# Attention scores of the last 64 keys as float32 64x64 products, with side work of the attention loop moved

## The chip, the cores and the metric

The kernel runs on one core of one Trainium2 chip. The metric is the device time of one execution in microseconds (us); lower is better. Three runs of the kernel before took 912.76 to 914.37 us, median 913.71 us. A profile of one further execution gives the trace that is read here.

## The reference

Attention with a sigmoid in place of the softmax, then a mixture-of-experts layer with greedy routing by capacity:

```python
B, H, S, D = 8, 12, 448, 64                       # float32 q, k, v
scores = q @ k.transpose(0, 1, 3, 2) / sqrt(D) - log(S)
attn_out = (1 / (1 + exp(-scores))) @ v           # per image and head
x = attn_out.transpose(0, 2, 1, 3).reshape(3584, 768)
logits = x @ w_gate                               # 8 experts
# (token, expert) pairs in the order of falling logits: a token goes to its
# first expert that has room; each expert takes 3584 / 8 = 448 tokens
for e in range(8):
    out[mask[e]] = relu(x[mask[e]] @ w1[e]) @ w2[e]   # 768 -> 1024 -> 768
```

## The kernel before

The program has three stages, one behind the other: attention with the gate's logits (to about 304 us of the profiled span), routing for the first expert (to about 358 us), and the experts' products, between which the routing for the later experts runs. All instructions are issued in the order of the code: each engine works through its own queue in that order and waits on semaphores. The change touches the first stage alone.

**The attention loop.** The work is cut into 48 pairs of heads (8 images of 6 pairs; "odd" and "even" below are by the pair's number in its image). Step `i` of the loop holds, in this order: `load` of the pairs `i+4` and `i+5` (even steps only), `turn` of pair `i+1`, the `scores` of pair `i`, up to two functions off the list `bg`, and `av` of pair `i-1`.

- `load(b, g)` issues the DMAs of four heads. For each of the two pairs, 4 DMAs bring k and 4 bring q into one tile `nkq` [128, 2, 448] (4 buffers), k from SP's queue and q from GpSimd's (POOL's); 6 more bring v (`nv`, `nr`; 3 buffers each). For the first two pairs q comes over ACT's queue and v over POOL's.
- `turn` is one 32x32 block transpose of k and q on DVE into `kqT` (float32; the partitions hold 2 heads of 64 channels, the two slots of the next axis are k and q). The function `split` that it returns makes the fp32r pair: `kqH` (rounded, ACT) and `kqL` (`kqT - kqH`, DVE). `split` is called behind the first scores of a step, so ACT does the first sigmoid `at`, then `kqH`, then the other sigmoids.
- `scores(c)` for 128 keys makes six fp32r products (high times high, high times low, low times high, for two heads on the two row halves of the array) into a tile `sc` of two PSUM banks (3 buffers), and ACT turns it into `at` (8 buffers) with one sigmoid of 896 columns.
- 448 keys are three and a half such groups. An odd pair makes a fourth tile, for the last 64 keys of two pairs: six products with the last 128 keys of the pair before, of which only the upper 64 rows stay, then six with the last 64 keys of its own over the lower 64 rows. So `kqH` and `kqL` of the pair before (2 buffers each) are read until the end of an odd step.
- `av` multiplies v with the sigmoids in plain float32 in the form 128x64 (`L441`), and for an odd pair the shared fourth tile with the last 64 rows of v, in the form 64x64 (`L447`), into the PSUM tiles `tp` (2 buffers). DVE copies the result to `xt` (`L449`) and for odd pairs adds the other part (`L451`).
- `bg` holds `logits` of a whole image (24 products 128x32, then an addition on DVE) and, for the first image only, 8 pieces `rows` (three transposes into `tp`, a copy on DVE, and behind every second piece a store). The rows of the other seven images come after the loop.
- `route_consts` makes the constants of the routing: 16 iotas and memsets on POOL and 25 small operations on DVE (shifts, comparisons, casts), all at the end of step 2, behind that step's `av`.

Of the kernel before, what the change touches and what calls it, by code (L numbers as in the profile page):

```python
# [47 lines left out]
def route_consts(nc, cp, K):  # L48
# [6 lines left out]
    nc.vector.tensor_scalar(t1, t1, 4, None, OP.logical_shift_right)  # L55
# [5 lines left out]
    nc.vector.tensor_scalar(K.G, t1, t10, None, OP.is_equal)
# [3 lines left out]
    nc.vector.tensor_scalar(K.TRI, ti, 128.5, None, OP.is_gt)  # L65
# [11 lines left out]
    nc.vector.tensor_copy(K.rank, t3)  # L77
# [254 lines left out]
def moe_attention(tc, q, k, v, w_gate, w1, w2, out):  # L332
# [7 lines left out]
    with contextlib.ExitStack() as ctx:  # L340
# [21 lines left out]
        def load(b, g, qq=nc.gpsimd, vq=nc.sync):  # L362


            nat["v", b, g] = ld.tile([128, G4, 3, D], F32, name="nv", bufs=3)
            nat["r", b, g] = ld.tile([128, 2, D], F32, name="nr", bufs=3)
            for i in range(2):
                t = nat["kq", b, 2 * g + i] = ld.tile([128, 2, S // 32, 32], F32, name="nkq", bufs=4)
                for n, (qn, src) in enumerate(((nc.sync, k), (qq, q))):
                    for j in range(2):  # L370
                        rws = src[b, g * G4 + 2 * i + j].rearrange("(c p) (x d) -> x p c d", p=32, x=2)
                        for x in range(2):
                            o = 64 * j + 32 * x
                            qn.dma_start(t[o:o + 32, n], rws[x])  # L374
# [11 lines left out]
        load(0, 0, nc.scalar, nc.gpsimd)  # L386
# [6 lines left out]
        KQ = {}  # L393
        def turn(b, pr):


            T = wk.tile([128, 2, S], F32, name="kqT")
            nc.vector.transpose(T.rearrange("p n t -> p (n t)"), nat["kq", b, pr].rearrange("p n c d -> p (n c d)"))  # L398
# [4 lines left out]
            def split():
                nc.scalar.activation(H, T, AF.Copy)  # L404
                nc.vector.tensor_tensor(L, T, H.bitcast(F32), OP.subtract)  # L405
            return split
# [3 lines left out]
        def products(p, b, pr, keys, m):  # L410


            KH, KL, QH, QL = KQ[b, pr]
            for i, (R, M) in enumerate(((KH, QH), (KH, QL), (KL, QH))):
                for j, half in enumerate((LO, HI)):
                    nc.tensor.matmul(p[:m, j, :S], R[half, keys], M[half], start=i == 0, stop=i == 2)  # L416

        def scores(b, pr, c):


# [7 lines left out]
            nc.scalar.activation(a, p[:, :, :S], AF.Sigmoid, bias=bias, scale=1 / math.sqrt(D))  # L428
# [376 lines left out]
```

## Time and profile before

| | before |
|---|---|
| runs, us | 912.76, 913.71, 914.37 |
| profiled execution, us | 915.77 |
| its span, first to last instruction, us | 914.0 |
| mean granted TensorE clock | 0.984 |
| busy PE / DVE / ACT / POOL | 94% / 59% / 50% / 51% |

| stretch of the span, us | PE busy | DVE busy | ACT busy | POOL busy | DMA share |
|---|---|---|---|---|---|
| 0 to 9 (first loads) | 0.18 | 1.32 | 2.33 | 8.20 | 0.96 |
| 9 to 304 (attention) | 286.07 | 151.73 | 198.22 | 117.61 | 0.56 |
| 304 to 398 (routing, first expert begins) | 72.62 | 80.25 | 46.22 | 28.71 | 0.59 |
| 398 to 914 (experts) | 501.81 | 301.83 | 210.90 | 309.14 | 0.39 |

A row of the timeline gives the start in us from the span's start, the duration, the engine, the line, the operation, the tiles (out<-in) and, in square brackets, the idle time of the engine before it and what ended that. One product in float32 is recorded as two matmuls, one in fp32r as one. Neighbours of one kind are merged into a row with a count; their durations overlap, so what a matmul costs is read from the distance between starts.

### The profile page before, as it was taken

What the parts mean: (1) busy time and instruction counts of PE and PEld (TensorE: products, weight loads), DVE (VectorE), ACT (ScalarE), POOL (GpSimd) and SP (SyncE); (2) the same over time, 40 slices, a digit from 0 to 9 for tenths busy, and PEclk for the clock granted to TensorE, in tenths of its full rate; (3) what the DMA queues carried; (4) which work ended last, traced back from release to release, by engine and by line L of the source; (5) the groups of instructions that cost most, each with busy time, mean ns of one, the idle gap of its engine ahead of it and who ended that gap; (6) DMA issues with size and microseconds to landing.
All of it is one profiled execution on the core that took longest, in us unless ns stands there. A gap on an engine that the chain in (4) does not pass through costs nothing.

```text
span 914.0 us, 16457 instructions
## 1 busy us (share of the span) xinstructions
PE 860.7 (94%) x5603; PEld 656.2 (72%) x5603; DVE 535.1 (59%) x2053; ACT 457.7 (50%) x633; POOL 463.7 (51%) x442
## 2 busy tenths in 40 slices
PE   5898999999999774998999999999999999999997
PEld 3444555555555444987998888988988888989996
DVE  3645455555554588876968969959779632330110
ACT  5565676676677472443433534534434434544441
POOL 8533444444430003573675675684784783741651
PEclk9999999999999996999899999999999999999999
DMA  9646665555550486324434343353452442632421
GB/s 176 140 97 149 126 128 117 116 125 118 116 121 1 127 277 185 108 82 149 140 114 146 122 147 124 128 151 113 154 162 96 141 154 90 213 117 82 158 76 61
DMA packets 205236, 117.59 MB, mean 129 GB/s; under 512 B 145728, under 2 KB 194880, under 8 KB 205152
## 3 DMA queue, kind: packets, MB, share of 16 engines
q1 hardware_dynamic: 190688, 83.03, 35.2%
q0 software_dynamic: 10752, 33.05, 11.4%
q10 hardware_dynamic: 3712, 0.46, 0.3%
q8 instruction: 44, 0.72, 0.3%
q14 instruction: 40, 0.33, 0.1%
HBM read 94.47 MB, written 22.02 MB: 127 GB/s over the span
## 4 chain that ended last, share of the span: by engine, by line
PE 78%; DVE 11%; issue 4%; DMA 2%; POOL 2%; ACT 2%; SPq 0%; POOLq 0%; ACTq 0%; DVEq 0%
PE sc L416 14%; PE tp L441 12%; PE sc L671 9%; PE sc L669 9%; PE sc L673 9%; PE sc L706 6%; PE sc L708 6%; PE sc L704 6%; DVE r_junk L170 3%; PE tp L447 2%; PE tp L634 2%; PE tp L621 2%; DMA xr<-xs,r_idx 1%; PE tp L462 1%; POOL wl L587 1%
## 5 line engine op out<-in xcount | busy, mean ns | idle before, releaser
L587 POOL TENSOR_TENSOR wl<-wr,wh 128x768 fp32r<-128x768 f32 (+1 forms) x96 | 205.7, 2151 | 135.5 <-ACT wh L585 124.6
L428 ACT ACTIVATE at<-sc,bias 128x896 f32<-128x896 f32 x168 | 160.6, 1003 | 63.2 <-PE sc L416 62.9
L374 POOL DMA_DIRECT2D nkq<-in_q_dram x184 | 115.5, 640 | 142.3 <-DVE kqT L398 132.9
L708 PE MATMUL sc<-hh,wl 128*128 128x448 f32 (+2 forms) x400 | 151.4, 379 | 0.0
L673 PE MATMUL sc<-xh,wl 128*128 128x448 f32 (+2 forms) x396 | 146.7, 370 | 0.0
L671 PE MATMUL sc<-xl,wh 128*128 128x448 f32 (+2 forms) x396 | 146.3, 370 | 0.0
L706 PE MATMUL sc<-hl,wh 128*128 128x448 f32 (+2 forms) x400 | 145.5, 364 | 0.2 <-POOL hl L681 0.2
L669 PE MATMUL sc<-xh,wh 128*128 128x448 f32 (+2 forms) x396 | 145.4, 367 | 0.0
L704 PE MATMUL sc<-hh,wh 128*128 128x448 f32 (+2 forms) x400 | 143.9, 360 | 0.0
L170 DVE TENSOR_SCALAR_CACHE_REDUCE r_junk<-r_KE,r_T 128x224 bf16<-128x224 f32 x315 | 123.3, 442 | 0.1
L441 PE MATMUL tp<-at,nv 128*64 128x448 f32 x576 | 118.8, 548 | 4.8 <-DVE xr L478 4.4
L585 ACT ACTIVATE wh<-wr 128x768 fp32r<-128x768 f32 (+1 forms) x112 | 102.0, 939 | 9.7 <-DMA wr<-in_moe_w_dram 9.7
L405 DVE TENSOR_TENSOR kqL<-kqT,kqH 128x896 fp32r<-128x896 f32 x48 | 52.4, 1092 | 68.5 <-ACT kqH L404 68.5
L681 POOL TENSOR_TENSOR hl<-yt,hh 128x896 fp32r<-128x896 f32 x32 | 68.2, 2132 | 46.7 <-ACT yt L680 45.1
L416 PE MATMUL sc<-kqH 64*128 64x448 f32 (+1 forms) x384 | 79.3, 410 | 11.7 <-ACT kqH L404 8.8
L677 ACT ACTIVATE hh<-sc 128x896 fp32r<-128x896 f32 x32 | 29.4, 919 | 111.5 <-PE sc L673 111.5
L441 PEld LDWEIGHTS tp<-at,nv 128*64 128x64 f32 x576 | 37.0, 136 | 63.7 <-issue 55.3
L706 PEld LDWEIGHTS sc<-hl,wh 128*128 128x128 f32 x400 | 75.2, 188 | 7.3 <-issue 1.1
L671 PEld LDWEIGHTS sc<-xl,wh 128*128 128x128 f32 x396 | 75.5, 191 | 6.5 <-issue 0.4
L669 PEld LDWEIGHTS sc<-xh,wh 128*128 128x128 f32 x396 | 75.7, 191 | 5.7
L607 POOL DMA_INDIRECT xr<-xs,r_idx x32 | 31.9, 997 | 94.0 <-ACT wh L585 83.2
L673 PEld LDWEIGHTS sc<-xh,wl 128*128 128x128 f32 x396 | 75.5, 191 | 5.0
(155 smaller groups left out, 1327.3 us busy)
## 6 DMA issues: line engine op xcount, KB each, us to landing
wr<-in_moe_w_dram SPq DMA_DIRECT2D x64, 384.0 KB, 3.0
wr<-in_moe_w_dram SPq DMA_DIRECT2D x48, 512.0 KB, 3.9
nkq<-in_k_dram SPq DMA_DIRECT2D x192, 56.0 KB, 2.5
xs<-xr SPq DMA_DIRECT2D x32, 336.0 KB, 3.3
nkq<-in_q_dram POOLq DMA_DIRECT2D x184, 56.0 KB, 2.6
nv<-in_v_dram SPq DMA_DIRECT2D x92, 96.0 KB, 2.4
nr<-in_v_dram SPq DMA_DIRECT2D x46, 32.0 KB, 2.3
xr<-xs,r_idx POOLq DMA_INDIRECT x32, 4.6
```

Of the source, the lines that this page charges most:

```text
L170: nc.vector.tensor_scalar(junk, KE, T[:, i:i + 1].bitcast(F32), None, OP.is_ge, OP.add, accum_out=cnt[:, i:i + 1])
L374: qn.dma_start(t[o:o + 32, n], rws[x])
L416: nc.tensor.matmul(p[:m, j, :S], R[half, keys], M[half], start=i == 0, stop=i == 2)
L428: nc.scalar.activation(a, p[:, :, :S], AF.Sigmoid, bias=bias, scale=1 / math.sqrt(D))
L441: nc.tensor.matmul(p[j * 64:j * 64 + 64, :S], nat["v", b, g][:, h0 + j, c, :], AT[b, pr, c][:, j, :], start=(c == 0), stop=(c == 2 and pr ...
L587: eng.tensor_tensor(lo, raw[u], hi.bitcast(F32), OP.subtract)
L669: nc.tensor.matmul(ph[:, f, lo:hi], wh[:, a, fs], xh[:, dd, lo:hi], start=st, stop=False)
L671: nc.tensor.matmul(ph[:, f, lo:hi], wh[:, a, fs], xl[:, dd, lo:hi], start=False, stop=False)
L673: nc.tensor.matmul(ph[:, f, lo:hi], wl[:, a, fs], xh[:, dd, lo:hi], start=False, stop=en)
L704: nc.tensor.matmul(py[:, d2, :w], wh[:, a, dsl], h1, start=st, stop=False)
L706: nc.tensor.matmul(py[:, d2, :w], wh[:, a, dsl], h2, start=False, stop=False)
L708: nc.tensor.matmul(py[:, d2, :w], wl[:, a, dsl], h1, start=False, stop=(j == 1 and a == 3))
```

## The change

Six things are done.

1. The fourth tile is made by a function of its own, `rest_scores`, from the float32 `kqT` of two pairs: four plain float32 products of 64 keys, one for each quarter of the array. It is called at the end of the even step before (behind that step's `av`), so its sigmoid stands on ACT between two steps. `kqT` gets 3 buffers in place of 2.
2. `bg` is worked off behind `av` (and behind `rest_scores`) in place of ahead of it, one function in each step in place of two.
3. `route_consts` is a generator: its POOL part runs in step 3, its DVE part in six pieces at the ends of steps 5 to 10.
4. The first pair's transpose, `kqH` and `kqL` are made in two halves (k, then q).
5. In the first `load`, q of the second pair comes over POOL's queue in place of ACT's, and there ahead of v.
6. With that, no step reads the `kqH` and `kqL` of the pair before any more.

```diff
@@ route_consts: all DVE operations now stand behind the POOL ones @@
+    yield
+    yield
+    nc.vector.tensor_scalar(t1, t1, 4, None, OP.logical_shift_right)
+    nc.vector.tensor_scalar(t9, t9, 4, None, OP.logical_shift_right)
+    nc.vector.tensor_copy(t10, t9)
+    yield
+    nc.vector.tensor_scalar(K.G, t1, t10, None, OP.is_equal)
+    nc.vector.tensor_scalar(K.TRI, ti, 128.5, None, OP.is_gt)
+    yield
+    nc.vector.tensor_copy(K.rank, t3)
...
+    yield
+    nc.vector.tensor_scalar(K.SEL, t6, t7, None, OP.is_equal)
     for st in range(1, 16):
...
+        if st % 5 == 0:
+            yield
@@ moe_attention @@
-        def load(b, g, qq=nc.gpsimd, vq=nc.sync):
+        def load(b, g, qq=(nc.gpsimd, nc.gpsimd), vq=nc.sync):
...
-                for n, (qn, src) in enumerate(((nc.sync, k), (qq, q))):
+                for n, (qn, src) in enumerate(((nc.sync, k), (qq[i], q))):
...
-        load(0, 0, nc.scalar, nc.gpsimd)
+        load(0, 0, (nc.scalar, nc.gpsimd), nc.gpsimd)
...
-        def turn(b, pr):
+        def turn(b, pr, cuts=((0, 2),)):
-            T = wk.tile([128, 2, S], F32, name="kqT")
-            nc.vector.transpose(T..., nat["kq", b, pr]...)
+            T = KT[b, pr] = wk.tile([128, 2, S], F32, name="kqT", bufs=3)
+            for x, y in cuts:
+                nc.vector.transpose(T[:, x:y]..., nat["kq", b, pr][:, x:y]...)
...
             def split():
-                nc.scalar.activation(H, T, AF.Copy)
-                nc.vector.tensor_tensor(L, T, H.bitcast(F32), OP.subtract)
+                for x, y in cuts:
+                    nc.scalar.activation(H[:, x:y], T[:, x:y], AF.Copy)
+                    nc.vector.tensor_tensor(L[:, x:y], T[:, x:y], H[:, x:y].bitcast(F32), OP.subtract)
...
-            if c < 3:
-                products(p, b, pr, slice(c * 128, c * 128 + 128), 128)
-            else:
-                products(p, b, pr - 1, slice(S - 128, S), 128)
-                products(p, b, pr, slice(S - 64, S), 64)
+        def rest_scores(b, pr):
+            a = AT[b, pr, 3] = wk.tile([128, 2, S], F32, name="at", bufs=AT_BUFS)
+            p = ps_s.tile([128, 2, 512], F32, name="sc")
+            for o, T in ((HI, KT[b, pr - 1]), (LO, KT[b, pr])):
+                for j, half in enumerate((LO, HI)):
+                    nc.tensor.matmul(p[o, j, :S], T[half, 0, S - 64:S], T[half, 1], start=True, stop=True)
+            sigmoid(a, p)
...
-        turn(*pairs[0])()
+        turn(*pairs[0], ((0, 1), (1, 2)))()
         bg, late = [], []
+        consts = route_consts(nc, cp, K)
...
-            for c in range(4 if cur and cur[1] % 2 else 3 if cur else 0):
+            for c in range(3 if cur else 0):
                 scores(*cur, c)
                 if c == 0 and split:
                     split()
-            for _ in range(2):
-                if bg:
-                    bg.pop(0)()
+            if bg and not cur:
+                bg.pop(0)()
             if old:
                 av(*old)
-            if i == 2:
-                route_consts(nc, cp, K)
+            if cur and cur[1] % 2 == 0:
+                rest_scores(*nxt)
+            if i > 2:
+                next(consts, None)
+            if bg and cur:
+                bg.pop(0)()
```

**Where the instructions stand, 1: TensorE (PE).** Step 7 of the kernel before (an odd pair: its first three score tiles, of which the last stands in the first three rows, then the fourth tile with `kqH_541` of the pair before and `kqH_623` of its own; the logits of image 0 and a piece of its rows; then `av`):

```order
L416 MATMUL sc_693<-kqH_623 128x448 x2
L416 MATMUL sc_693<-kqL_624,kqH_623 128x448 x2
L416 MATMUL sc_693<-kqH_623,kqL_624 128x448 x2
L416 MATMUL sc_702<-kqH_541 128x448 x2
L416 MATMUL sc_702<-kqL_542,kqH_541 128x448 x2
L416 MATMUL sc_702<-kqH_541,kqL_542 128x448 x2
L416 MATMUL sc_702<-kqH_623 64x448 x2
L416 MATMUL sc_702<-kqL_624,kqH_623 64x448 x2
L416 MATMUL sc_702<-kqH_623,kqL_624 64x448 x2
L462 MATMUL tp_716<-xt_265,wgz_84 32x112 x24
L473 MATMUL tp_743<-ident_81,xt_265 112x128 x3
L441 MATMUL tp_749<-at_625,nv_274 64x448 x2
```

The end of step 8 of the kernel after (an even pair: the last score tile's last rows would stand ahead; here the last of `av`, its 64x64 part, the new fourth tile of step 9, a piece of rows, and the first scores of step 9):

```order
L455 MATMUL tp_765<-at_657,nv_269 64x448 x2
L461 MATMUL tp_772<-at_624,nr_270 64x448
L461 MATMUL tp_765<-at_624,nr_270 64x448
L461 MATMUL tp_772<-at_624,nr_270 64x448
L461 MATMUL tp_765<-at_624,nr_270 64x448
L441 MATMUL sc_780<-kqT_633 64x448 x2
L441 MATMUL sc_780<-kqT_732 64x448 x2
L487 MATMUL tp_793<-ident_81,xt_260 112x128 x3
L431 MATMUL sc_803<-kqH_734 128x448 x2
L431 MATMUL sc_803<-kqL_735,kqH_734 128x448 x2
L431 MATMUL sc_803<-kqH_734,kqL_735 128x448 x2
```

Twelve fp32r products ahead of an odd pair's `av` are gone; four float32 products stand behind an even step's 64x64 part of `av`, and the side work stands behind them.

**2: ScalarE (ACT)** from the start of the program, before (q's DMAs for pairs 0 and 1, the table load, then `kqH` and sigmoids of the steps 0 and 1):

```order
L374 DMA nkq_94<-in_q_dram 32x14x32 x4
L374 DMA nkq_103<-in_q_dram 32x14x32 x4
L387 ACT_TABLE_LOAD
L387 ACTIVATE warm_85<-warm_85 1x1
L404 ACTIVATE kqH_154<-kqT_152 128x896
L428 ACTIVATE at_188<-sc_189,bias_82 128x896
L404 ACTIVATE kqH_186<-kqT_184 128x896
L428 ACTIVATE at_199<-sc_200,bias_82 128x896
L428 ACTIVATE at_208<-sc_209,bias_82 128x896
L428 ACTIVATE at_221<-sc_222,bias_82 128x896
L404 ACTIVATE kqH_219<-kqT_217 128x896
```

And after:

```order
L381 DMA nkq_94<-in_q_dram 32x14x32 x4
L394 ACT_TABLE_LOAD
L394 ACTIVATE warm_85<-warm_85 1x1
L414 ACTIVATE kqH_155<-kqT_152 128x448 x2
L421 ACTIVATE at_191<-sc_192,bias_82 128x896
L414 ACTIVATE kqH_189<-kqT_187 128x896
L421 ACTIVATE at_202<-sc_203,bias_82 128x896
L421 ACTIVATE at_211<-sc_212,bias_82 128x896
L421 ACTIVATE at_220<-sc_221,bias_82 128x896
L421 ACTIVATE at_231<-sc_232,bias_82 128x896
L414 ACTIVATE kqH_229<-kqT_227 128x896
```

Four DMAs are gone from ACT's queue, and `at_220`, the fourth tile's sigmoid, now stands ahead of the first sigmoid and of `kqH` of the odd step (`at_231`, `kqH_229`).

**3: VectorE (DVE)**, the end of step 2 and the start of step 3, before (the copies of `av`, then constants, the first ones and the last, and the transpose for pair 4):

```order
L449 COPY xt_265<-tp_333 128x448
L451 TENSOR_TENSOR xt_265<-tp_340,xt_265 128x448
L55 TENSOR_SCALAR c_t1_350<-c_t1_350 128x128
L59 TENSOR_SCALAR c_t9_353<-c_t9_353 128x1
L60 CAST c_t10_354<-c_t9_353 128x1
L61 TENSOR_SCALAR c_G_347<-c_t1_350,c_t10_354 128x128
L65 TENSOR_SCALAR c_TRI_361<-c_ti_348 128x128
```

After, the same place and the steps 3 to 5:

```order
L463 COPY xt_260<-tp_328 128x448
L465 TENSOR_TENSOR xt_260<-tp_335,xt_260 128x448
L406 STREAM_TRANSPOSE kqT_349<-nkq_163 128x896
L415 TENSOR_TENSOR kqL_352<-kqT_349,kqH_351 128x896
L463 COPY xt_260<-tp_382 128x448
L406 STREAM_TRANSPOSE kqT_453<-nkq_172 128x896
L415 TENSOR_TENSOR kqL_456<-kqT_453,kqH_455 128x896
L463 COPY xt_260<-tp_486 128x448
L465 TENSOR_TENSOR xt_260<-tp_493,xt_260 128x448
L406 STREAM_TRANSPOSE kqT_507<-nkq_271 128x896
L415 TENSOR_TENSOR kqL_510<-kqT_507,kqH_509 128x896
L463 COPY xt_260<-tp_540 128x448
```

No constant stands between the copies of step 2 and the next transpose any more.

More of the change, by code (lines that the diff above doesn't have):

```diff
@@ L54, in route_consts @@
     nc.gpsimd.iota(t1, [[1, 128]], base=0, channel_multiplier=0)
-    nc.vector.tensor_scalar(t1, t1, 4, None, OP.logical_shift_right)
     t9 = cp.tile([128, 1], I32, name="c_t9")
@@ L64, in route_consts @@
     K.TRI = cp.tile([128, 128], BF, name="c_TRI")
-    nc.vector.tensor_scalar(K.TRI, ti, 128.5, None, OP.is_gt)
     K.ones = cp.tile([128, 1], BF, name="c_ones")
@@ L76, in route_consts @@
     nc.gpsimd.iota(t3, [[-1, 8]], base=8, channel_multiplier=0)
-    nc.vector.tensor_copy(K.rank, t3)
     K.tok = cp.tile([112, 32], F16, name="c_tok")
@@ L90, in route_consts @@
     nc.gpsimd.iota(t5, [[0, 1]], base=0, channel_multiplier=1)
-    nc.vector.tensor_scalar(t5, t5, 31, None, OP.bitwise_and)
     nc.gpsimd.iota(t6, [[1, 2], [2, 4]], base=0, channel_multiplier=0)
-    t7 = cp.tile([128, 1], F32, name="c_t7")
-    nc.vector.tensor_copy(t7, t5)
-    nc.vector.tensor_scalar(K.SEL, t6, t7, None, OP.is_equal)
     K.kk = cp.tile([128, 16, 3], I32, name="c_kk")
@@ L99, in route_consts @@
     nc.gpsimd.iota(t8, [[1, 3]], base=1, channel_multiplier=0)
+    K.c0 = cp.tile([128, 3], I32, name="c_c0")
+    for i, u in enumerate((0xBFFFFFFF, 0x00000000, 0x40000000)):
+        nc.gpsimd.memset(K.c0[:, i:i + 1], _s32(u))
+    yield
[8 more added lines that the diff above has]
+    nc.vector.tensor_copy(K.rank, t3)
+    nc.vector.tensor_copy(K.tok, t4)
+    nc.vector.tensor_scalar(t5, t5, 31, None, OP.bitwise_and)
+    t7 = cp.tile([128, 1], F32, name="c_t7")
+    nc.vector.tensor_copy(t7, t5)
+    yield
+    nc.vector.tensor_scalar(K.SEL, t6, t7, None, OP.is_equal)
     g = 0
@@ L104, in route_consts @@
         g ^= (0x4B000000 << sh) & 0xFFFFFFFF
+        if st % 5 == 0:
+            yield
     K.gfin = _s32(g)
-    K.c0 = cp.tile([128, 3], I32, name="c_c0")
-    for i, u in enumerate((0xBFFFFFFF, 0x00000000, 0x40000000)):
-        nc.gpsimd.memset(K.c0[:, i:i + 1], _s32(u))
 class Router:
@@ L391, in moe_attention @@
             nc.sync.dma_start(wgz[:, :, s, 8 * s:8 * s + 8], w_gate.rearrange("(c p) e -> p c e", p=128))
-        KQ = {}
-        def turn(b, pr):
-            T = wk.tile([128, 2, S], F32, name="kqT")
-            nc.vector.transpose(T.rearrange("p n t -> p (n t)"), nat["kq", b, pr].rearrange("p n c d -> p (n c d)"))
+        KQ, KT = {}, {}
+        def turn(b, pr, cuts=((0, 2),)):
+            T = KT[b, pr] = wk.tile([128, 2, S], F32, name="kqT", bufs=3)
+            for x, y in cuts:
+                nc.vector.transpose(T[:, x:y].rearrange("p n t -> p (n t)"),
+                                    nat["kq", b, pr][:, x:y].rearrange("p n c d -> p (n c d)"))
             H = wk.tile([128, 2, S], F32R, name="kqH")
@@ L403, in split, with sigmoid, scores @@
             def split():
-                nc.scalar.activation(H, T, AF.Copy)
-                nc.vector.tensor_tensor(L, T, H.bitcast(F32), OP.subtract)
+                for x, y in cuts:
+                    nc.scalar.activation(H[:, x:y], T[:, x:y], AF.Copy)
+                    nc.vector.tensor_tensor(L[:, x:y], T[:, x:y], H[:, x:y].bitcast(F32), OP.subtract)
             return split
         AT = {}
-        def products(p, b, pr, keys, m):
+        def sigmoid(a, p):
+            nc.scalar.activation(a, p[:, :, :S], AF.Sigmoid, bias=bias, scale=1 / math.sqrt(D))
+        def scores(b, pr, c):
+            a = AT[b, pr, c] = wk.tile([128, 2, S], F32, name="at", bufs=AT_BUFS)
+            p = ps_s.tile([128, 2, 512], F32, name="sc")
             KH, KL, QH, QL = KQ[b, pr]
@@ L415, in products @@
                 for j, half in enumerate((LO, HI)):
-                    nc.tensor.matmul(p[:m, j, :S], R[half, keys], M[half], start=i == 0, stop=i == 2)
-        def scores(b, pr, c):
-            a = AT[b, pr, c] = wk.tile([128, 2, S], F32, name="at", bufs=AT_BUFS)
+                    nc.tensor.matmul(p[:, j, :S], R[half, c * 128:(c + 1) * 128], M[half], start=i == 0, stop=i == 2)
+            sigmoid(a, p)
+        def rest_scores(b, pr):
+            a = AT[b, pr, 3] = wk.tile([128, 2, S], F32, name="at", bufs=AT_BUFS)
             p = ps_s.tile([128, 2, 512], F32, name="sc")
-            if c < 3:
-                products(p, b, pr, slice(c * 128, c * 128 + 128), 128)
-            else:
-                products(p, b, pr - 1, slice(S - 128, S), 128)
-                products(p, b, pr, slice(S - 64, S), 64)
-            nc.scalar.activation(a, p[:, :, :S], AF.Sigmoid, bias=bias, scale=1 / math.sqrt(D))
+            for o, T in ((HI, KT[b, pr - 1]), (LO, KT[b, pr])):
+                for j, half in enumerate((LO, HI)):
+                    nc.tensor.matmul(p[o, j, :S], T[half, 0, S - 64:S], T[half, 1], start=True, stop=True)
+            sigmoid(a, p)
         XT = {}
```

4 lines of the change are left out of this document (removed).

## The prediction

> **What bounds the kernel now.** First the page: how busy TensorE is, and whose work makes the chain that ended last.
>
> ```profile
> span 914.0 us, 16457 instructions
> ...
> PE 860.7 (94%) x5603; PEld 656.2 (72%) x5603; DVE 535.1 (59%) x2053; ACT 457.7 (50%) x633; POOL 463.7 (51%) x442
> ...
> PE   5898999999999774998999999999999999999997
> ...
> PE 78%; DVE 11%; issue 4%; DMA 2%; POOL 2%; ACT 2%; SPq 0%; POOLq 0%; ACTq 0%; DVEq 0%
> ```
>
> PE carries 78% of the chain, and the slices of the attention stage (the first 13) are full of it, but for the first. So a step of the attention loop lasts as long as PE's queue for it, and I priced the change from distances between PE's starts. Next came the timeline of one odd and one even step:
>
> ```profile
> 153.91 0.47 PE L416 MATMUL sc<-kqH 64*128 64x448 f32 x2
> ...
> 155.66 0.37 PE L416 MATMUL sc<-kqH,kqL 64*128 64x448 f32 x2
> ...
> 155.95 0.47 PE L416 MATMUL sc<-kqH 64*128 64x448 f32 x2
> ...
> 157.36 2.48 PE L441 MATMUL tp<-at,nv 128*64 128x448 f32 x12
> ...
> 159.76 0.47 PE L416 MATMUL sc<-kqH 64*128 64x448 f32 x2
> ...
> 160.74 1.01 ACT L428 ACTIVATE at<-sc,bias 128x896 f32<-128x896 f32 x1 [0.18 <-PE sc L416]
> ...
> 161.49 0.36 PE L416 MATMUL sc<-kqH,kqL 64*128 64x448 f32 x2
> ...
> 161.78 2.48 PE L441 MATMUL tp<-at,nv 128*64 128x448 f32 x12
> ...
> 161.91 0.95 ACT L404 ACTIVATE kqH<-kqT 128x896 fp32r<-128x896 f32 x1 [0.16 <-ACT at L428]
> ...
> 162.89 1.09 DVE L405 TENSOR_TENSOR kqL<-kqT,kqH 128x896 fp32r<-128x896 f32 x1 [1.37 <-ACT kqH L404]
> ...
> 164.19 0.98 PE L447 MATMUL tp<-at,nr 64*64 64x448 f32 x8
> ...
> 165.10 0.47 PE L416 MATMUL sc<-kqH 64*128 64x448 f32 x2
> ```
>
> The odd step runs from 153.91 to 159.76 (5.85), the even one to 165.10 (5.34); in the odd one the fourth tile lies between 155.95 and 157.36. In the even one, three score tiles take 2.02 (to 161.78), `av` 2.41, the 64x64 part 0.91.
>
> **The fourth tile.** Without it an odd step is three score tiles and `av`: 2.02 + 2.40 (157.36 to 159.76) = 4.42, so 5.85 − 4.42 = 1.43 goes. Its replacement has no row of its own, but `L447` has its form: four float32 products 64x64, two for each row half, two for each column half, 448 columns, the row halves writing different banks. All four take 0.91 with the change of form on both sides. Their inner distance:
>
> ```profile
> 153.00 0.98 PE L447 MATMUL tp<-at,nr 64*64 64x448 f32 x8
> ...
> 153.42 0.56 PE L447 MATMUL tp<-at,nr 64*64 64x448 f32 x4
> ...
> 154.05 0.62 DVE L449 COPY xt<-tp 128x448 f32<-128x448 f32 x1 [1.53 <-PE tp L447]
> ...
> 155.12 1.10 DVE L398 STREAM_TRANSPOSE kqT<-nkq 128x896 f32<-128x896 f32 x1
> ```
>
> The second four of eight records start 0.42 after the first, and the next scores 0.49 after those. Standing right behind `L447` in the same form, the new tile needs two such distances: 2 × 0.42 = 0.84 at most, 2 × 0.375 = 0.75 if it goes on like `av`, whose six distances fill 2.25 of its 2.40. I take 0.80; the ends for the range are 0.75 and 0.91. Each of 24 double steps changes by 0.80 − 1.43 = −0.63; one of them lies in the start below, so 23 × 0.63 = **−14.5**.
>
> Does anything take PE's place? Let an odd step begin at 0. ACT now has the fourth tile's sigmoid first: it can start some 0.2 behind the last product and ends at 1.2; the first sigmoid (ready at 0.98, as 160.74 − 159.76) ends at 2.15; `kqH` (0.95) ends at 3.2 with its gap of 0.16; `kqL` (1.09) at 4.35. The transpose it needs ends at about 1.6: in the rows the copy starts 0.14 behind the 64x64 part and the transpose ends 2.17 after that, and 0.75 of this lies behind the new tile. The next step begins at 4.42, and `kqL` is wanted 0.31 later (its second kind of product): 0.4 to spare. ACT's load in a double step, seven sigmoids and two `kqH` at 0.95 to 1.01, is at most 9 of 10.56. The `sc` buffer that the third score tile wants, 1.33 into the odd step, is freed at 1.2. SP and POOL get no more DMAs in the loop; k and q come three pairs ahead. All hidden, the narrowest cover being that 0.4.
>
> **The constants.** The timeline around step 2, whose end holds them:
>
> ```profile
> 25.14 0.47 PE L416 MATMUL sc<-kqH 64*128 64x448 f32 x2
> ...
> 26.35 2.14 DVE L55 TENSOR_SCALAR c_t<-c_t 128x128 int32<-128x128 int32 x1
> ...
> 27.28 1.00 POOL L85 MEMSET c_mv<- 112x1024 f16 x1
> ...
> 28.74 0.29 DVE L61 TENSOR_SCALAR c_G<-c_t,c_t 128x128 bf16<-128x128 int32 x1
> ...
> 30.86 1.10 DVE L398 STREAM_TRANSPOSE kqT<-nkq 128x896 f32<-128x896 f32 x1
> ...
> 33.98 0.64 PE L416 MATMUL sc<-kqH 64*128 64x448 f32 x2 [2.92 <-ACT at L428]
> ...
> 37.54 2.48 PE L441 MATMUL tp<-at,nv 128*64 128x448 f32 x12
> ...
> 40.86 0.47 PE L416 MATMUL sc<-kqH 64*128 64x448 f32 x2
> ```
>
> From 26.35 to 30.86 DVE does constants, the transpose comes late, and PE stands idle for 2.92 before the scores at 33.98. That step lasts 33.98 − 25.14 = 8.84 in place of 5.85. The step behind it lasts 6.88 in place of 5.34, all of it in its scores, which need 3.56 in place of 2.02: PE is slow again after the pause. Both losses, 2.99 + 1.54, should go: **−4.5**. The new pieces hold at most three operations of 0.29 or six small ones, some 0.6 per step, behind copies where DVE has 0.5 or more before `kqH` wants the transpose; I cost them at nothing, and if that cover is short, at 0.1 to 0.3 in each of six steps.
>
> [...] The operation of 2.14 us ends just after POOL's memset (27.28 + 1.00), while one of the same size takes 0.29. [...]
>
> [...]
>
> ```profile
> L374 POOL DMA_DIRECT2D nkq<-in_q_dram x184 | 115.5, 640 | 142.3 <-DVE kqT L398 132.9
> ```
>
> **Logits and rows.** The five steps with the first image's side work:
>
> ```profile
> 52.05 0.47 PE L416 MATMUL sc<-kqH 64*128 64x448 f32 x2
> ...
> 55.50 1.36 PE L462 MATMUL tp<-xt,wgz 128*32 128x112 f32 x48
> 56.79 0.54 PE L473 MATMUL tp<-ident,xt 128*112 128x128 f32 x3
> ...
> 87.10 0.54 PE L473 MATMUL tp<-ident,xt 128*112 128x128 f32 x3
> 87.57 2.48 PE L441 MATMUL tp<-at,nv 128*64 128x448 f32 x12
> 89.98 0.48 PE L416 MATMUL sc<-kqH 64*128 64x448 f32 x2
> ```
>
> ```profile
> PE tp L441 <- DVE xr L478: 4.4, 3, 1.6
> ```
>
> They take 37.93; three plain odd and two plain even steps would take 3 × 5.85 + 2 × 5.34 = 28.23. Of the other 9.70, logits are 1.29 (55.50 to 56.79) and eight rows at 0.47 (87.10 to 87.57) are 3.76; 4.65 is waiting, and the waits table names it: `av` wants a `tp` buffer that a copy of rows still holds. Behind `av`, one piece a step, the copy has the next step's scores (2.02) to finish in. In an even step the piece itself may have to wait for the copy of the first `tp`, which ends 0.76 behind the 64x64 part, covered by the new tile's 0.80. I leave 0.05 for each of eight: **−4.2** (3.0 to 4.65). Logits of all images cost the same 1.29 behind `av` as ahead of it.
>
> **The start.**
>
> ```profile
> 6.28 1.11 DVE L398 STREAM_TRANSPOSE kqT<-nkq 128x896 f32<-128x896 f32 x1 [6.28 <-DMA nkq<-in_q_dram]
> ...
> 8.82 0.74 PE L416 MATMUL sc<-kqH 64*128 64x448 f32 x2 [8.82 <-ACT kqH L404]
> ...
> 10.32 1.11 DVE L398 STREAM_TRANSPOSE kqT<-nkq 128x896 f32<-128x896 f32 x1 [0.44 <-DMA nkq<-in_k_dram]
> ...
> 19.80 0.47 PE L416 MATMUL sc<-kqH 64*128 64x448 f32 x2
> ```
>
> The first transpose waits for q. In halves the k part runs before that, so from 6.28 there remain half a transpose (0.55) and half a `kqH` (0.47), with the hand-overs about 7.7 in place of 8.82. But pair 1's transpose at 10.32 waits for k while the DMA engines are full (share 0.96 up to 9 us), and the change issues k no earlier; it then gates `kqH`, the fourth tile and step 1. Going on by these durations (ACT: `kqH` to 12.4, three sigmoids and the fourth to 16.2, `kqH` to 17.1; PE's `av` from 15.95) I get step 2 at 18.5 in place of 19.80: **−1.3**, between −2.5 (k lands earlier, as ACT's queue is done sooner) and +1.5 (pair 2's q, now behind pair 1's 4 DMAs and v on POOL, lands late).
>
> **Sum.** 14.5 + 4.5 + 4.2 + 1.3 = 24.5, none of it in the later stages, which begin that much earlier with the same work. The profiled execution took 915.77 (1.77 outside its span of 914.0), 2.06 above the median of the runs; the span should come to 889.5, and the time, from the median of 913.71, to 889.2. I say 889.3.
>
> **The rivals.**
> - *`kqL` late in odd steps.* Speaking for it: only 0.4 to spare behind a sigmoid that was not there. If `kqH` slips by one more activation (0.95), each of 23 odd steps stalls by 0.55: +12.7, 902. Against: each duration in that sum is measured. Half of such a slip gives about 891 to 896.
> - *The four products share the array only in pairs*, like `av` (0.40 for each two records): 1.60, +0.17 per double step in place of −0.63; 23 × 0.80 = 18.4 above the forecast, 907.7. Against: `L447`.
> - *Slower than before: the four run one behind another.* Eight records at 0.40 make 3.20; the double step grows by 1.77, 24 × 1.77 = 42.5, less the 10.0 of the other parts: 946. It decides from 1.43 + 10.0 / 24 = 1.85 per tile on. For it, only that these operands, `kqT` twice, have never been read so; against, that `L447` has 0.91 in all its 24 places.
> - *The start gains nothing or loses 1.5*: 890.5 to 892.
> [...]
>
> **How the numbers follow.** Forecast 0.66, late `kqL` 0.13, pairs 0.03, one by one 0.03, start 0.09, constants 0.06. The forecast's own range is 886.5 (tile at 0.75: 15.7; rows 4.65; constants 4.5; start 2.5) to 893 (tile at 0.84, rows 3.0, start 0). Start and constants lie inside it; with the milder half of the late `kqL` and a tile at 0.91 the range becomes 886 to 896.5 and leaves out somewhat under 2 in 10. A measurement of this kernel can tell about 0.2%, 1.8 us, from no change: faster 0.95, same 0.02, slower 0.03.
>
> **What would show it.** In the profile after: even steps of about 6.1 and odd ones of 4.4, the four `kqT` products taking 0.75 to 0.85; no idle PE near 31 to 34 us and no slow scores behind it; no wait of `av` for a copy of rows; step 2's scores at 18 to 19 us; the attention's last 64x64 part near 279 us in place of 303. It is wrong if odd steps wait for `kqL`, if the `kqT` products start more than 0.45 apart, or if the routing behind gives time back.

## The result, and the profile after

Four runs of the changed kernel took 886.94 to 890.47 us, median 888.97; the kernel before took 914.04 beside them (912.76 to 914.58). The ratio is 0.9726, 95% interval 0.97 to 0.9752. The forecast was 889.3.

The profiled execution took 887.7 us. From its page: span and counts, the busy engines, PE's 40 slices, and the shares of the chain that ended last.

```profile
span 885.9 us, 16254 instructions
...
PE 843.1 (95%) x5507; PEld 638.0 (72%) x5507; DVE 534.8 (60%) x2055; ACT 457.1 (52%) x634; POOL 466.1 (53%) x446
...
PE   6999999999998739998999999999999999999996
...
PE 79%; DVE 11%; issue 5%; POOL 3%; DMA 1%; ACT 0%; SPq 0%; POOLq 0%; DVEq 0%
```

PE's work fell by 17.6 us (860.7 before), and its share of the chain stayed where it was. The dip inside the first slices is gone. The attention stage ended 26.1 us earlier: its last 64x64 part of `av` starts at 302.54 in the kernel before and at 276.42 after. The stretches behind it, cut 26.1 earlier than in the table of before (the columns are length, then busy PE, PEld, DVE, ACT and POOL, granted clock, DMA share, GB/s):

```profile
277.90:371.90 94.00, 72.76 (x472) 58.21 (x473) 80.41 (x430) 46.43 (x84) 28.87 (x19) 0.91 0.59 185
371.90:885.90 514.00, 500.15 (x2821) 442.71 (x2819) 301.59 (x1419) 210.99 (x331) 309.03 (x208) 0.99 0.40 127
```

Routing has the same busy times as before. The experts end 2.0 us earlier in this trace, but from the first expert's product to the end all the traces of this study lie between 551.3 and 555.4, with the same code there: scatter. So the rest of this text goes by where attention ends. The medians differ by 25.1.

One odd and one even step of the timeline after:

```profile
158.96 0.47 PE L431 MATMUL sc<-kqH 64*128 64x448 f32 x2
159.18 1.91 ACT L421 ACTIVATE at<-sc,bias 128x896 f32<-128x896 f32 x2 [1.75 <-PE sc L441]
...
160.24 0.19 PEld L431 LDWEIGHTS sc<-kqH 64*128 64x128 f32 x2 [0.17 <-ACT at L421]
160.28 0.42 PE L431 MATMUL sc<-kqH 64*128 64x448 f32 x2
...
160.97 0.95 ACT L414 ACTIVATE kqH<-kqT 128x896 fp32r<-128x896 f32 x1
...
161.95 1.09 DVE L415 TENSOR_TENSOR kqL<-kqT,kqH 128x896 fp32r<-128x896 f32 x1 [1.43 <-ACT kqH L414]
...
163.44 0.47 PE L431 MATMUL sc<-kqH 64*128 64x448 f32 x2
163.75 0.36 PE L431 MATMUL sc<-kqL,kqH 64*128 64x448 f32 x2
...
167.87 0.98 PE L461 MATMUL tp<-at,nr 64*64 64x448 f32 x8
168.67 0.93 PE L441 MATMUL sc<-kqT 64*64 64x448 f32 x8
169.53 0.47 PE L431 MATMUL sc<-kqH 64*128 64x448 f32 x2
```

The odd step takes 4.48, the even one 6.09, together 10.57 (10.58 as a mean; 11.19 before). The four `kqT` products start 0.80 behind the 64x64 part of `av`, and the next scores 0.86 behind them.

The constants and the rows, in the timeline:

```profile
27.50 0.47 PE L431 MATMUL sc<-kqH 64*128 64x448 f32 x2
...
33.59 0.47 PE L431 MATMUL sc<-kqH 64*128 64x448 f32 x2
...
38.73 0.22 DVE L94 TENSOR_SCALAR c_t<-c_t 128x128 int32<-128x128 int32 x1
...
49.94 0.47 PE L431 MATMUL sc<-kqH 64*128 64x448 f32 x2
...
56.10 0.54 PE L487 MATMUL tp<-ident,xt 128*112 128x128 f32 x3
56.57 0.47 PE L431 MATMUL sc<-kqH 64*128 64x448 f32 x2
```

Step 4 runs from 27.50 to 33.59, a plain even step; the constant that took 2.14 before takes 0.22. Step 8, with a piece of rows, takes 6.63, that is 0.54 above a plain one, and PE has no idle time ahead of its transposes. The waits table has no row for `av` waiting on a copy of rows any more.

The start:

```profile
0.77 8.42 SPq L381 DMA_DIRECT2D nkq<-in_k_dram  x16
...
2.85 1.28 ACT L394 ACT_TABLE_LOAD   x1 [2.85 <-issue]
...
7.21 0.74 PE L431 MATMUL sc<-kqH 64*128 64x448 f32 x2 [7.21 <-ACT kqH L414]
7.74 1.10 DVE L406 STREAM_TRANSPOSE kqT<-nkq 128x896 f32<-128x896 f32 x1
...
8.79 0.57 PE L431 MATMUL sc<-kqH 64*128 64x448 f32 x2
9.17 0.57 PE L431 MATMUL sc<-kqL,kqH 64*128 64x448 f32 x2
...
11.16 0.98 PE L441 MATMUL sc<-kqT 64*64 64x448 f32 x8
...
16.91 0.47 PE L431 MATMUL sc<-kqH 64*128 64x448 f32 x2
```

The first product is 1.61 earlier than before, pair 1's transpose 2.58, and step 2's scores 2.89 (16.91 for 19.80). ACT's table load, which stood behind eight DMA issues and began at 6.43 in the kernel before, begins at 2.85 (SPq is SP's queue of DMA issues). PE's first products lie 0.37 apart (8.79 to 9.17); the tile at 11.16 has its usual length, and from there on the distance is 0.20.

### The profile page after: what moved, and what is told of

Read it like the earlier page. It is cut to its first block, busy times and chain, and to the rows that moved or that the text cites. A ratio compares the mean times of both kernels' runs of the same rounds, so it can differ in the third digit from the quotient of the medians.

```text
span 885.9 us, 16254 instructions
## 1 busy us (share of the span) xinstructions
PE 843.1 (95%) x5507; PEld 638.0 (72%) x5507; DVE 534.8 (60%) x2055; ACT 457.1 (52%) x634; POOL 466.1 (53%) x446
## 4 chain that ended last, share of the span: by engine, by line
PE 79%; DVE 11%; issue 5%; POOL 3%; DMA 1%; ACT 0%; SPq 0%; POOLq 0%; DVEq 0%
PE tp L455 13%; PE sc L431 11%; PE sc L689 8%; PE sc L687 8%; PE sc L691 8%; PE sc L724 6%; PE sc L726 6%; PE sc L722 6%; DVE r_junk L177 4%; PE tp L461 2%; PE sc L441 2%; PE tp L652 2%; PE tp L639 2%; POOL wl L605 1%; POOL hl L699 1%
## 5 line engine op out<-in xcount | busy, mean ns | idle before, releaser
L381 POOL DMA_DIRECT2D nkq<-in_q_dram x188 | 118.3, 645 | 115.9 <-DVE kqT L406 102.5
L415 DVE TENSOR_TENSOR kqL<-kqT,kqH 128x896 fp32r<-128x896 f32 (+1 forms) x49 | 52.5, 1073 | 58.5 <-ACT kqH L414 58.3
L605 DVE TENSOR_TENSOR wl<-wr,wh 128x768 fp32r<-128x768 f32 (+1 forms) x16 | 25.0, 1567 | 91.7 <-ACT wh L603 85.5
L722 PEld LDWEIGHTS sc<-hh,wh 128*128 128x128 f32 x400 | 75.6, 189 | 4.6
```

Source lines behind the costliest of these rows:

```text
L605: eng.tensor_tensor(lo, raw[u], hi.bitcast(F32), OP.subtract)
L722: nc.tensor.matmul(py[:, d2, :w], wh[:, a, dsl], h1, start=st, stop=False)
```

## The experiments

In each, "attention ends" is the start of the last of the 64x64 products of `av`, 303.0 before and 276.9 after; ratios are against the kernel before, run on the same chip.

### The tile by itself, and the tile twice

`tile_only` is the kernel before with the new tile alone (`rest_scores` behind `av` in even steps, three `kqT` buffers). `tile_twice` is the kernel after with every product of the tile issued twice:

```diff
-            for o, T in ((HI, KT[b, pr - 1]), (LO, KT[b, pr])):
+            for o, T in ((HI, KT[b, pr - 1]), (LO, KT[b, pr])) * 2:
```

> The kernel before with the fourth tile alone (four float32 64x64 products behind the even step's av); side work, constants and start as before. Theory (the tile is worth the difference of PE distances, 0.61 per double step in the trace after): 24 x 0.61 = 14.6 less than before, about 899.4 us; odd steps 4.4 to 4.5, even ones 6.1, the last 64x64 part of av near 288 us in place of 302.5; the pause at 31 to 34 us stays. Rival (the gain of the tile needs the side work and the constants out of the way, because odd steps have little cover): less than 10 gained, odd steps with side work longer than before by more than their work.

Measured: 901.92 us, ratio 0.9848 [0.9829, 0.9868]; attention ends at 288.7, 14.3 earlier. Plain steps take 4.48 and 6.09. The pause at the constants stays (steps 3 and 4 are 3.56 above plain ones), and so do the waits at the rows: `av` waits 4.8 in its row of the waits table, where before had 4.4. So the tile's gain doesn't need the other parts: the rival's bound of 10 is passed, though the attention stage gained 0.3 less than the 14.6 expected.

> The kernel after with the four float32 products of the fourth tile issued twice (same result, twice the work). Theory (the four share the array, two passes of 0.375 to 0.42): even steps longer by 0.75 to 0.84, 24 x 0.8 = 19 slower than after, about 908 us. Rival (they share it only in pairs, the overlap seen in the 0.81 being that with their neighbours): even steps longer by 1.5 to 1.6, 38 slower, 927 us. Second rival (PE has slack that hides part): under 15 slower.

Measured: 907.5 us, ratio 0.9903 [0.9883, 0.9923]; attention ends 17.7 later than after, 0.74 for each of 24 tiles. The timeline of an even step's end:

```profile
119.71 1.68 PE L441 MATMUL sc<-kqT 64*64 64x448 f32 x16
121.32 0.47 PE L431 MATMUL sc<-kqH 64*128 64x448 f32 x2
```

From 119.71 to 121.32 eight products take 1.61, where four took 0.86: four more cost 0.75, which is two passes of 0.375. So all four do share the array, one in each quarter; by the prediction's prices, sharing in pairs would have cost 1.60 and one behind another 3.20.

### The constants put back, and put early

`consts_back` makes all constants at the end of step 2, as before, with the rest of the change kept. `consts_pool_early` does the POOL part at the end of step 0 and the whole DVE part at the end of step 2.

```diff
@@ consts_back @@
-            if i > 2:
-                next(consts, None)
+            if i == 2:
+                for _ in consts:
+                    pass
@@ consts_pool_early @@
-            if i > 2:
-                next(consts, None)
+            if i == 0:
+                next(consts)
+            if i == 2:
+                for _ in consts:
+                    pass
```

> The kernel after with both parts of the constants at the end of step 2 again, in one piece. Theory (DVE waits for GpSimd's iota and memset, the transpose comes late, PE pauses and is slow behind the pause): step 3 longer by about 3, step 4 by 1.5, 4.5 in all: 893.5 us. Rival (with shorter steps the same delay costs more, since the steps hold less cover): 5.5 or more, 894.5 us and up. Rival (constants cost little, the gain came from elsewhere): under 2.

Measured: 897.48 us, ratio 0.9807 [0.9791, 0.9824]; attention ends at 285.3, 8.4 later than after. From the timelines of DVE, POOL and PE:

```profile
25.00 3.59 DVE L94 TENSOR_SCALAR c_t<-c_t 128x128 int32<-128x128 int32 x1 [1.36 <-POOL c_t L54]
25.02 2.14 POOL L65 IOTA c_io<- 112x2048 int16 x1
27.38 1.04 POOL L78 MEMSET c_mv<- 112x1024 f16 x1
...
33.16 0.74 PE L431 MATMUL sc<-kqH 64*128 64x448 f32 x2 [5.49 <-ACT kqH L414]
```

The first operation spans POOL's long iota and the memset behind it and takes 3.59. In the kernel before it began at 26.35, took 2.14, and ended just behind the memset too (28.49, for 28.59 here). Both times this is where POOL's whole series of iotas and memsets comes to its end: the last group, of three small memsets, starts at 28.45 before and at 28.55 here. Other work of DVE isn't held so: in the kernel after, `kqL` (25.99, 1.09) and the copy of `av` (27.62, 0.62) keep their usual lengths beside the same series. PE pauses for 5.49 in place of 2.92. Step 3 is 5.56 and step 4 2.69 above a plain step, 8.25 together, where before lost 4.5 to the same operations. That is what the rival with less cover expected (5.5 or more), and the rows agree with it: POOL begins its constants at 24.47, as before at 24.37, since its q issues stand ahead of them, while step 3 begins at 23.10 in place of 25.14, and a plain odd step is 1.36 shorter.

> The kernel after with GpSimd's part of the constants at the end of step 0 and all of DVE's part in one piece at the end of step 2. Theory (of the 4.5 us for which DVE held the transpose back, 2.1 was waiting for GpSimd's iota and memset): the first operation takes 0.2 to 0.3 in place of 2.14, DVE holds the transpose back 2.4, PE pauses about 0.5 to 1.5 and stays fast, 1 slower than after: 890 us. Rival (the operations take that long by themselves): the first two again 2 us, the pause 3, slow products behind it, 893.5 us.

Measured: 888.71 us, ratio 0.9718 [0.9702, 0.9734]; attention ends at 279.0, 2.1 later than after, which the times don't tell apart.

```profile
23.66 0.22 DVE L94 TENSOR_SCALAR c_t<-c_t 128x128 int32<-128x128 int32 x1
23.69 10.23 POOL L381 DMA_DIRECT2D nkq<-in_q_dram  x16
26.29 1.10 DVE L406 STREAM_TRANSPOSE kqT<-nkq 128x896 f32<-128x896 f32 x1
```

The same DVE work in one block, but beside POOL's q issues and not beside its iota and memset, is done in 2.6 us (23.66 to 26.29). The delayed transpose then costs 0.79 and 0.92 in steps 3 and 4, 1.7 in all; PE pauses for 0.71 and its products keep their distance of 0.20 behind that. So of the 8.25 the length of the DVE block itself is worth 1.7; the rest goes with the operation held up beside POOL and with the slow products after the pause.

### The side work ahead of av again

`side_ahead` keeps everything but the place of `bg`: two functions a step, ahead of `av`.

```diff
-            if bg and not cur:
-                bg.pop(0)()
+            for _ in range(2):
+                if bg:
+                    bg.pop(0)()
...
-            if bg and cur:
-                bg.pop(0)()
```

> The kernel after with logits and rows ahead of av again, two pieces a step. Theory (av waits for a tp buffer that the copy of rows holds): the five steps 7 to 11 longer by 4.0 to 4.7 in sum than the eight pieces cost now, 893.4 us. Rival (the wait is hidden once steps are shorter, or goes to the DVE transposes): under 2.5, or over 6.

Measured: 898.59 us, ratio 0.9819 [0.9803, 0.9835]; attention ends at 287.1, 10.2 later than after. Of this 0.7 lies in the start (step 2 at 17.57); steps 7 to 11 are 14.64 above plain ones, of which 1.29 are logits and 3.8 rows, so 9.5 were lost to waiting and what follows it, where before lost 4.65. The theory expected 4.0 to 4.7, and it had the wait right but not its size, which is over the rival's 6. First a row of the timeline, then one of the waits (total, times, longest), then a window:

```profile
56.72 3.75 PE L455 MATMUL tp<-at,nv 128*64 128x448 f32 x12 [2.28 <-DVE xr L492]
```

```profile
PE tp L455 <- DVE xr L492: 6.0, 3, 2.3
```

```profile
59.00:61.00 2.00, 2.00 (x8) 0.31 (x9) 0.00 (x0) 0.00 (x0) 0.00 (x0) 0.50 0.00 0
```

The waits total 6.0 (4.4 before); the largest is 2.28, and behind it `av` takes 3.75 in place of 2.48 at a granted clock of 0.50 from 59 to 61. A pause of 1.88 in step 10 is followed by an `av` of 4.17, while behind one of 1.79 in step 9 `av` keeps its 2.48. Part of the loss is therefore PE's speed after the pause: the slow products of steps 8 and 10 come to some 3.3 of the 9.5. Why the waits themselves are longer than before isn't shown.

### The start: one half of the change each, and PE warmed first

`start_queue_only` undoes the halves, `start_halves_only` puts q of pair 1 back on ACT's queue. `warm_start` adds products of the identity with itself at PE's head, while the first loads run.

```diff
@@ start_queue_only @@
-        turn(*pairs[0], ((0, 1), (1, 2)))()
+        turn(*pairs[0])()
@@ start_halves_only @@
-        load(0, 0, (nc.scalar, nc.gpsimd), nc.gpsimd)
+        load(0, 0, (nc.scalar, nc.scalar), nc.gpsimd)
@@ warm_start @@
+        p = ps_t.tile([128, 512], F32, name="tp")
+        for _ in range(13):
+            nc.tensor.matmul(p[:, :128], ident, ident, start=True, stop=True)
```

> The kernel after with the first pair's transpose, kqH and kqL in one piece again; q of pair 1 still on GpSimd's queue. Theory (the halves are worth the 1.0 to 1.1 by which the first product moved, but step 1 is gated by pair 1's k, which the shorter ACT queue let land earlier): first product at 8.2 to 8.4, step 2's first scores at 17.0 to 17.8 in place of 16.91, 0.3 to 0.9 slower than after, 889.5 us. Rival (the halves carry the start's gain): step 2 at 18.5 or later, 1.6 slower.

Measured: 889.36 us, ratio 0.973 [0.9713, 0.9746]; attention ends at 279.0 (+2.1).

```profile
0.77 8.48 SPq L381 DMA_DIRECT2D nkq<-in_k_dram  x16
...
8.67 0.74 PE L431 MATMUL sc<-kqH 64*128 64x448 f32 x2 [8.67 <-ACT kqH L414]
...
13.08 1.68 PE L441 MATMUL sc<-kqT 64*64 64x448 f32 x8
...
19.12 0.47 PE L431 MATMUL sc<-kqH 64*128 64x448 f32 x2
```

> The kernel after with q of pair 1 back on ACT's queue; halves kept. Theory (ACT's table load and pair 1's k wait behind ACT's four more DMAs): pair 1's transpose near 10 in place of 7.74, step 2's first scores at 18.4 to 19, 1.5 to 2 slower than after, 890.7 us. Rival (the queue does not matter, halves do): step 2 at 17.2 or earlier, under 0.4 slower.

Measured: 890.36 us, ratio 0.9742 [0.9725, 0.9758]; attention ends at 279.2 (+2.3).

```profile
0.77 10.26 SPq L381 DMA_DIRECT2D nkq<-in_k_dram  x16
...
6.27 1.28 ACT L394 ACT_TABLE_LOAD   x1 [6.27 <-DMA nkq<-in_q_dram]
...
8.75 0.74 PE L431 MATMUL sc<-kqH 64*128 64x448 f32 x2 [8.75 <-ACT kqH L414]
10.34 1.11 DVE L406 STREAM_TRANSPOSE kqT<-nkq 128x896 f32<-128x896 f32 x1 [0.91 <-DMA nkq<-in_k_dram]
...
19.26 0.47 PE L431 MATMUL sc<-kqH 64*128 64x448 f32 x2
```

Step 2 starts at 19.12 and 19.26, in both kernels later than the theory had it; with the new tile alone it starts at 19.17. Each part by itself gains nothing, both together 2.26. They are two gates in a row. Without the halves the first transpose starts at 6.53 in place of 5.38, the first product comes at 8.67, and pair 1's transpose, which stands behind the first `kqL` on DVE, starts at 9.66 in place of 7.74. Without the queue ACT's table load, behind four more DMA issues, starts at 6.27 in place of 2.85, so `kqH` starts at 7.67 in place of 6.06 (first product at 8.75 though the halves are there), and k of pair 1 comes late (10.34). In both kernels the products also keep their double distances until 14.7 and 15.1; in the kernel after they end at about 11.2. That is the smaller part: in `side_ahead`, with the start of the kernel after, they lasted to 13.4 and step 2 still started at 17.57. The slow stretch is about as long there (6.2) as in these two kernels (6.0 and 6.4), so some 1.55 (19.12 − 17.57) of the 2.2 goes to the two gates and up to 0.66 to the moment when PE becomes fast.

> The kernel after with 13 extra float32 products of the 128x128 identity at the head of PE's queue, while the first loads are under way; their result is used nowhere. Theory (the first scores go at 0.37 a distance in place of 0.20 because PE is slow after a pause, as behind the pause of the constants): the first products at 0.20, first sigmoid 0.5 to 0.8 earlier, step 1 and 2 begin 0.5 to 1.5 earlier than in after (12.1 and 16.9), about 887.3 us. Rival (ACT's queue and the loads gate the start, PE's speed is hidden): the products fast, step 2 unmoved, same time as after. Rival (the extra products do not speed PE up): distances stay 0.37.

Measured: 889.39 us, ratio 0.9722 [0.97, 0.9745]; attention ends at 276.9, as after.

```profile
13.78 1.11 DVE L409 STREAM_TRANSPOSE kqT<-nkq 128x896 f32<-128x896 f32 x1 [2.22 <-DMA nv<-in_v_dram]
```

The products of step 0 are 0.20 apart from 8.12 us on and step 1 starts 0.69 earlier (11.39 for 12.08), but pair 2's transpose waits 2.22 for loads, and step 3 starts where it did (23.03 for 23.0). In step 2 the loads set the pace. So the theory was right about the products and the rival about the time.

### The covers: kqL later, and the tile in the middle

`split_late` makes `kqH` of the next pair behind the second sigmoid in odd steps. `tile_mid` issues the tile between the two forms of `av` (128x64, tile, 64x64), so that its sigmoid is ready 0.8 earlier.

```diff
@@ split_late @@
-                if c == 0 and split:
+                if c == cur[1] % 2 and split:
@@ tile_mid: av calls its new argument mid ahead of its 64x64 part @@
+            if mid:
+                mid()
...
+            rest = (lambda: rest_scores(*nxt)) if cur and cur[1] % 2 == 0 else None
             if old:
-                av(*old)
-            if cur and cur[1] % 2 == 0:
-                rest_scores(*nxt)
+                av(*old, rest)
+            elif rest:
+                rest()
```

> The kernel after with kqH and kqL of an odd step behind its second sigmoid in place of its first, so kqH starts one activation (0.95) later. By the prediction's cover of 0.4: each odd step longer by 0.55, 12.7 slower, 901.7 us. By the trace after, where kqL of step 3 ends at 27.08 and is wanted at 27.81 (0.73 of cover): longer by 0.2 to 0.3, 5 to 7 slower, 895 us. Rival (no cover problem, PE's queue alone counts): within 1 of after.

Measured: 891.9 us, ratio 0.9757 [0.974, 0.9774]; attention ends at 281.6 (+4.7).

```profile
27.55 1.09 DVE L415 TENSOR_TENSOR kqL<-kqT,kqH 128x896 fp32r<-128x896 f32 x1 [2.33 <-ACT kqH L414]
28.16 0.47 PE L431 MATMUL sc<-kqH 64*128 64x448 f32 x2
28.69 0.47 PE L431 MATMUL sc<-kqL,kqH 64*128 64x448 f32 x2
```

`kqL` ends at 28.64 and its first product starts 0.53 behind the first `kqH` product; without a wait that distance is 0.31. Even steps behind a plain odd step grow by 0.26 to 0.38; those behind an odd step with logits or a piece of rows keep their length, since the side work covers the delay.

> The kernel after with the fourth tile's four products between the 128x64 and the 64x64 part of the even step's av in place of behind it. Theory (in the trace after, odd steps last 4.49 in place of 4.42 since their third score tile waits 0.07 for the buffer that the fourth tile's sigmoid frees; 0.8 earlier, that wait goes and kqL has more cover): odd steps 4.42, 23 x 0.07 = 1.6 faster than after, 887.4 us. Rival (the 64x64 part of av is now 0.8 later, so DVE's copy, the next transpose and kqH are later too, and odd steps wait for kqL): odd steps longer than 4.49, the same time as after or slower.

Measured: 892.3 us, ratio 0.9761 [0.974, 0.9782]; attention ends at 280.0 (+3.1). Odd steps fall to 4.42, as expected, since the third score tile no longer waits 0.07 for the `sc` buffer of the fourth; but the attention stage gets longer, and not by the rival's cause: each of the five even steps with side work grows by nearly 0.8.

```profile
56.98 0.54 PE L489 MATMUL tp<-ident,xt 128*112 128x128 f32 x3 [0.77 <-DVE xt L465]
```

The transposes of a piece need a `tp` buffer that the copy of `av` still holds. Standing behind the 64x64 part, the tile had covered that copy.

### The kernel after again, and the best version

`after_again` is the kernel after, unchanged. `both_better` is `warm_start` with the tile in the middle only in even steps that have no side work.

> The kernel after itself, unchanged, as the reference for the other runs on this chip: 886 to 891 us. Every theory expects the same; it prices what one run against another can tell (predicted: the later stages differ by up to 2 between executions).

Measured: 888.08 us, ratio 0.9701 [0.9679, 0.9722]; attention ends at 277.1, step 2 starts at 17.2.

> The kernel with those 13 products, and the fourth tile between the two parts of av in even steps without side work only (behind av in the steps with logits or rows). Theory (the middle place wins 0.07 in each odd step and lost 0.77 in the five even steps with side work alone, because the tile no longer covered DVE's copy): odd steps 4.42, even steps with rows 6.63, 19 x 0.07 = 1.3 less than warm_start, about 886 us. Rival (the middle place costs elsewhere, as by a later transpose): odd steps above 4.45 or the attention's end no earlier than in warm_start.

Measured: 887.92 us, ratio 0.9714 [0.9694, 0.9734]; attention ends at 275.9, 1.0 earlier than in `warm_start`. Odd steps take 4.43, even ones with rows 6.63 again. It is the shortest attention of all, but its time isn't told apart from that of the kernel after.

## Why the prediction was right, step by step

| term, us | forecast | measured, from the traces |
|---|---|---|
| fourth tile, 23 double steps | −14.5 | 23 × (10.58 − 11.19) = −14.0 |
| constants | −4.5 | steps 3 and 4 at 4.50 and 6.09: −4.5 |
| rows | −4.2 | 8 pieces cost 4 × 0.54 + 4 × 0.41 = 3.8 in place of 9.70 − 1.29 = 8.41: −4.6 |
| start | −1.3 | 19.80 to 16.91: −2.9 |
| sum | −24.5 | −26.0, attention ended 26.1 earlier |

- **The tile** was sized from `L447`, and that held: even steps came to 6.09 where 5.34 + 0.80 = 6.14 was forecast. Odd steps came to 4.48 in place of 4.42. There the forecast called the `sc` buffer of the third score tile hidden, freed at 1.2 and wanted at 1.33; in the rows the weight load (PEld) of that tile's first product waits 0.17 for a sigmoid of ACT (160.24). It is the fourth tile's, which starts 0.22 into the step and lasts about 1.0. The first product still starts 1.32 into the step, but the second stands 0.27 behind it in place of 0.20. `tile_mid`, where that sigmoid is earlier, has 4.42. A cover of 0.1 was none.
- **Late `kqL`.** The forecast had 0.4 to spare. In the rows it is there at 163.04 and wanted at 163.75: 0.71. `split_late` decides: with one activation more, a cover of 0.4 would have cost 0.55 a step and 12.7 in all, one of 0.71 some 0.25; measured were 0.26 to 0.38, in the steps that side work doesn't cover, and 4.7 in all. The forecast's cover was 0.3 too small because it put `kqH` at 2.25 into the step, with a gap of 0.16 ahead of it that is not there: it starts at 2.01 (160.97); the rest is the odd step, 0.06 longer than forecast.
- **Pairs, or one behind another:** refuted by the rows, and the doubling shows two passes.
- **The constants** gave exactly what was read from steps 3 and 4. That it must be these operations is shown by `consts_back`, which also shows that 4.5 isn't a property of the block: the same operations cost 8.25 when they began a little earlier against POOL. No run shows the wait to which the forecast gave its 0.06 for the constants: the six pieces of the kernel after cost no step anything. They don't run beside POOL's q issues (0.64 each in the kernel before), though: each stands between two groups of four; the first runs from 38.73 to 39.2, POOL's issues end at 37.94 and start again at 40.82. A wait for such issues is put to the test by `consts_pool_early`, where the whole block runs beside them and its operations take 0.14 to 0.30 each, as in the kernel after: there is none. Beside iota and memset the first operation took 2.14 (before) and 3.59 (`consts_back`). Both times it ended (28.49 and 28.59) only where POOL's whole series of them came to its end; what holds it there isn't shown.
- **The rows:** the term was 0.4 too small, since I left 0.05 of wait on each of eight pieces; on average there is none: a piece costs 0.54 in an even step, where its transposes start at 56.10, right behind the end of the copy at 56.04, and 0.41 in an odd one. So the cover in even steps is all used, with next to nothing to spare. The reason it gave, that the tile covers the copy, is shown by `tile_mid`, which takes the cover away and gets a wait of 0.77.
- **The start** is the step that failed: −2.9, outside its own ends of −2.5 and +1.5. It assumed that k of pair 1 lands no earlier because SP issues k as before. SP's 16 issues took 10.40 us (before) and 10.26 (`start_halves_only`) with eight q DMAs on ACT, and 8.42 and 8.48 with four, so k came earlier without being moved: pair 1's transpose starts at 7.74 and not at 10.32. It left out that ACT's table load stood behind the eight q issues: in the kernel before it ended at 7.71 and `kqH` followed at 7.83, though the first transpose had ended at 7.39; in the kernel after it ends at 4.13, and the first product comes at 7.21 where about 7.7 was forecast. It also kept the moment at which PE becomes fast where it had been. Of the 2.89, 0.63 come with the new tile (19.17 in `tile_only`); of the other 2.26, some 1.55 belong to the loads and the halves, and up to 0.66 to that moment. The kernel before, at its start:

```profile
6.43 1.28 ACT L387 ACT_TABLE_LOAD   x1 [6.43 <-DMA nkq<-in_q_dram]
...
7.83 0.93 ACT L404 ACTIVATE kqH<-kqT 128x896 fp32r<-128x896 f32 x1
```

The medians moved by 25.1 where the sum of measured terms is 26.0; the rest is inside the scatter of the later stages. The mechanisms of the three large terms held, but that the forecast of 889.3 lies 0.3 from the measured median is in part luck: the start gave 1.6 more than forecast and the rows 0.4, the tile 0.5 less, and that scatter hid most of the difference.

## What to carry to other kernels

Price a change on a full engine by distances between its starts, in the form and at the place where the new work will stand, and look for the operation in the same form that is already there. A wait on PE can cost more than its length, because the products behind it may be slow (in `side_ahead` waits of 6.0 went with a loss of 9.5, of which slow products were some 3.3); take out the pause itself and read the steps behind it too. Work put between a producer and its copy is also a cover: before moving it, ask which buffer that copy frees and who asks for it next, as the tile between the two forms showed.

## What the hardware showed that I had not expected

- **Short pauses slow PE.** After pauses of 2.92 (before) and 5.49 us (`consts_back`) the products stood 0.37 apart in place of 0.20, at a granted clock of 0.52 from 34.0 to 37.5 in the kernel before and of 0.50 from 33 to 37 in `consts_back`; after pauses of 1.88 and 2.28 (`side_ahead`) `av` took 4.17 and 3.75 in place of 2.48, behind the second at a granted clock of 0.50 from 59 to 61. After pauses of 1.28 to 1.58 (before) and 1.79 us (`side_ahead`) it kept its 2.48. What decides behind which pauses PE is slow, and for how long, isn't shown.
- **At the program's start the clock record says nothing of it.** In the kernel after, the window with the first products reads 1.00 while they stand 0.37 apart:

```profile
7.20:11.00 3.80, 3.79 (x18) 2.76 (x18) 1.67 (x4) 1.90 (x3) 3.80 (x7) 1.00 1.07 221
```

- **When the fast distances begin varies.** They began 4.0 us behind the first product in the kernel after and 6.2 in `side_ahead`, whose start is the same code (7.22 to 13.4); step 2 started at 16.91 and 17.57. Why isn't shown.
- **SP's issues took longer with more DMAs on ACT's queue.** The 16 k issues took 10.40 us (before) and 10.26 (`start_halves_only`) with eight q DMAs on ACT's queue, and 8.42 (after), 8.48 (`start_queue_only`), 8.55 (`both_better`) and 8.56 (`warm_start`) with four. By what they are slowed isn't shown.
